# Another early order for all five engines of a routed attention and expert kernel, with a few early copies on other engines

## The chip, the cores and the metric

The kernel runs on one core of a Trainium2 chip. The core has five engines that run their own instruction lists in order and meet through semaphores: PE (TensorE, matmuls; its weight loads are shown apart as PEld), DVE (VectorE), ACT (ScalarE), POOL (GpSimd) and SP (SyncE, which here issues DMAs). The metric is device time in microseconds of one launch; a launch before the change took 225.79 us (median of 3 runs, 225.51 to 225.9).

## The reference

Attention in which a query sees only keys of its own cluster, then an expert layer on the result. Batch 4, 8 heads, 768 tokens, head size 64, 16 clusters; the expert layer takes 3072 tokens of 512 to 1024 and back.

```
q_assign = argmax(einsum('bhsd,hcd->bhsc', q_n, c_n))     # q_n, k_n, c_n: normalised rows
k_assign = argmax(einsum('bhsd,hcd->bhsc', k_n, c_n))
mask   = q_assign[:, :, :, None] == k_assign[:, :, None, :]
scores = where(mask, scale * q @ k.T, -1e9)
attn   = exp(scores - max);  attn = attn / (sum(attn) + 1e-9)
x      = (attn @ v).transpose(0, 2, 1, 3).reshape(3072, 512)
h      = x @ w_in
solu   = h * softmax(h)
out    = ((solu - mean) / sqrt(var + 1e-6) * g_ln) @ w_out
```

## The kernel before

Work goes by pairs of heads: b.p is batch b, pair p (two heads of 64 rows make 128 partitions), sixteen in all. For each pair queries (i = 0) and keys (i = 1) are loaded, turned so that the head dimension lies on partitions, cast to bf16 into a ring of six buffers qk (L469 ACT, L471 and L473 POOL or DVE), and 16 rows below them take the one-hot of each token's cluster, so that one matmul gives a score that is large only within a cluster. Pairs of batch 0 are loaded twelve tokens to a partition and turned by PE (tp, L404) and copied out of PSUM (xa, L431); pair 0.0 goes in two halves (L397, L423). In pairs 0.1 to 0.3 two tokens are interleaved, which the kernel calls two-token. Pairs of later batches are loaded in four pieces each (L437) and turned by DVE (xt, L445).

Clusters of a pair come in these steps, each a name in the tables: cl (PE, four matmuls, L487), tb (DVE, transpose back, L493), mx (DVE, maximum, L506), oh (DVE, compare, L519), ot (DVE, turn the one-hot, L525 for two-token pairs, L528 else), pl (place it in qk; L541 for two-token pairs, L548 else; four of them, keys 1.0 and 1.1 and queries 0.0 and 0.1) and bl (zeroes, L557). For two-token pairs cl is one pass of all 384 columns.

Attention: S is a bank of scores (PE, L635), E its exp (ACT, L643, nine buffers), V the product with the values (PE, L662, six matmuls), N the normalisation of a group of V (DVE, L674 and L687). Values are loaded by lv (L561) and cast by cv (L566). S0 to S3 are pair 0.0, S4 to S21 pairs 0.1 to 0.3, S22 is the first of batch 1.

Expert layer, by tiles f of 128 tokens: tx turns x (DMA, for tile 0 by PE as ptx0, L727, and a copy tx0), h is x @ w_in (L752; h0.0.0 the first), hm its maximum (DVE, L758), ex the exp (ACT, L764), u the product (DVE, L771), tu turns u (DMA), bn and ag the statistics (DVE), y the product with w_out (PE, L821; y0.0 the first), sc and ou the output. Weights before that: li and wi load and cast w_in (L586), lo loads w_out, su0 to su7 add its eight blocks, weighted by g_ln (DVE, L603 and L606), me0 and me1 take the column mean of that sum (PE, L612), ce0 to ce7 subtract it (DVE, L615).

The order of every engine is written out by hand. A table ORDER has one string for each engine: `E3 ex E11` means three E, one ex, eleven E, each time the next operation of that kind which belongs to this engine. A second table, AWAY, names operations that run on another engine than their default. `queues` takes the lists from these, and `run` records the operations so; it also has a cost model, but the order within an engine is the table's alone.

```
for kind, n in re.findall(r"([A-Za-z]+)(\d*)", text):
    for _ in range(int(n or 1)):
        queues[e].append(of[e, kind].pop(0))
```

Needs between operations (`needs` in each `add`) become semaphore waits. An engine that meets a wait stops there: nothing behind it in its list runs.

Of the kernel before, what the change touches and what calls it, by code (L numbers as in the profile page):

```python
# [22 lines left out]
class Weave:  # L23
# [5 lines left out]
    ORDER["SP"] = """
        ld4 si ld3 lv lg ld2 lv lo ld lv2 lo ld10 lo2 ld2 li4 ld4 lv ld tx ld2 tx ld lv tu ld10 tx  # L30
        tu ld4 tu lv ld ou lv ld3 tu ld3 ou ld8 ou2 ld2 tu ld5 tx lv2 ld pl tu ld10 tx ld5 ou2 tu lv
        tx lv tu ld9 ou tu ld4 lv2 ld4 pl tu ou tx ld3 tu tx ld4 ou tu2 ou lv tx lv ou pl3 tu3 ou
        tx2 ou2 tu tx tu tx tu ou2 tx ou tu2 ou tu ou6
    """
# [7 lines left out]
    ORDER["PE"] = """
        fl wm tp2 cp fl3 tp cl tp fl tp fl4 cl tp3 fl S2 cq tp S2 cl S2 tp S2 tp S tp S gt V3 S tp S
        cl V3 S2 tp S2 tp S3 tp S V S V2 S7 V2 S V S2 cl S2 V2 S V S3 V S3 V3 S V S2 cl S4 V2 S V2
        S4 V4 S5 me V S2 V2 S V me S3 V S ptx V3 S3 V S2 V h2 V S V S h S2 h S V S V S V2 cl S3 V2
        h2 S V S h V S h S h S h V S2 V2 S y3 V S2 y S h2 S2 V2 h2 S2 cl S V S V2 S V S h S2 h S V S
        V S h y4 S3 V3 h2 S2 V2 S h S2 V y S y3 S2 V2 S cl S V S V S V2 S2 y S y S2 V3 S2 y S V S y
        S2 V2 S h S2 V3 S2 cl S V3 S3 cl S2 V2 S V2 S h2 S3 h V S V S V2 y3 S2 y V S2 V h S2 V S h S
        V S h2 S3 h V2 S2 V4 h S3 y3 S2 V y S2 V3 S2 h2 S3 V2 cl S3 V2 h S2 h cl V2 S2 V2 S h S2 h2
        S2 V3 y S y S y S y V S V2 S h2 S2 h2 S3 V3 S V y3 V y V S2 h S cl S3 V2 h S2 h V S2 V S cl  # L50
        V2 S3 y2 S V S V y2 h2 S2 V2 S h2 S3 cl S V3 S V S2 y3 S2 V y V S h S2 h V2 S h2 S3 h V2 S
        y2 S V2 S2 V2 y2 S2 h3 S3 V2 h2 V y S3 y3 V3 S3 h2 S2 cl S V S V S V2 S y2 h V S2 h V S2 h2
        S2 V S V h V4 S2 y2 h S3 V2 h2 S2 V2 S y2 S2 h2 y2 S h2 S2 V2 y S V2 S y h2 S3 h2 S2 V4 y S3
        h2 y V S2 h2 V S V S V y4 S2 V h4 S3 y V3 y S2 y2 h4 y S V3 y V y2 h ptx h y h2 y3 h2 y4 h2
        ptu2 y8 ptu y4 ptu y4
    """
    ORDER["DVE"] = """
        cn xb cb ca tb mx oh ot pl2 tb mx oh bl cf ot xa bl tb pl xa mx gk xa oh ot cv pl tb mx N oh
        xa2 su cv ot su2 N tb xt mx oh N xt su ot N pl tb mx su N su3 N oh xt ot N ce2 tx N ce5 N xt
        hm N ce u tb mx bn N hm oh bn ot ag u xt2 hm cv N bn u bn2 tb mx hm bn N oh ag2 u ot xt2 hm  # L60
        bn N sc u bn tb ag cv N xt mx oh xt ot sc N bl xt2 tb bn N mx ca tb N mx oh ot hm oh N ot u
        xt bn3 ag xt N ag hm sc N ca u bn2 xt bl sc hm ag N xt tb mx u tb oh ot N hm mx xt oh u bn2
        ot N hm bn ag xt ca u N bn tb xt2 mx ag hm tb N bn2 oh ot u xt2 N hm tb mx oh N ag bn bl u
        mx bn ot N bn oh hm ot ag xt u N bn xt ag hm bn2 ag u sc N bl hm ca tb mx cv2 oh u ot N bn2
        hm N bl u cv ag bn2 hm N bn u sc hm N u bn2 hm N bn ag u bn sc hm ag N bn u bn2 hm bn N ag2
        u bn2 hm ag bn N ag2 u tx bn hm sc u bn2 hm tu2 bn ag2 u2 bn2 ag tu sc
    """
# [16 lines left out]
    AWAY.update(dict.fromkeys("""
        ca0.0.1.1.0 ca0.0.1.1.1 pl0.0.0.0.0 pl0.0.0.1.0 pl0.0.1.1.0 pl1.0.0.0 pl1.0.0.1 pl1.0.1.0
        pl1.0.1.1 pl1.1.0.0 pl1.1.0.1 pl1.1.1.0 pl1.1.1.1 pl1.2.0.0 pl1.2.0.1 pl1.2.1.0 pl1.2.1.1
        pl1.3.0.0 pl1.3.0.1 pl1.3.1.0 pl1.3.1.1 pl2.0.0.0 pl2.0.0.1 pl2.0.1.0 pl2.0.1.1 pl2.1.0.0
        pl2.1.0.1 pl2.1.1.0 pl2.2.0.0 pl2.2.0.1 pl2.2.1.0 pl2.2.1.1 pl2.3.0.0 pl2.3.0.1 pl2.3.1.0
        pl2.3.1.1 pl3.0.0.0 pl3.0.0.1 pl3.0.1.0 pl3.1.0.0 pl3.1.0.1 pl3.1.1.0 pl3.1.1.1 pl3.2.0.0
        pl3.2.0.1 pl3.2.1.0 pl3.2.1.1 pl3.3.0.0  # L90
    """.split(), "POOL"))
# [1238 lines left out]
```

## Time and profile before

| | |
|---|---|
| time, median of 3 runs | 225.79 us (225.51 to 225.9) |
| profiled execution, its own time | 224.72 us |
| span of the profile | 222.9 us |
| ACT: exps, L643 | 142.7 us in 276 |
| PE: scores, L635 | 89.0 us in 600 |
| PE: values, L662 | 55.0 us in 1152 |
| PE: x @ w_in, L752 | 48.4 us in 177 |
| PE: u @ w_out, L821 | 45.1 us in 169 |

The span runs from the first to the last instruction; the time of the execution has what lies around it, 1.8 us here. Busy time is the sum over instructions, where overlaps count once. A row of a timeline has start, length, engine, line, operation and tiles, and in brackets the idle time of the engine just before it with what ended it. A wait for several semaphores is put down to the one that came last.

### The profile page before, as it was taken

What the parts mean: (1) busy time and instruction counts of PE and PEld (TensorE: products, weight loads), DVE (VectorE), ACT (ScalarE), POOL (GpSimd) and SP (SyncE); (2) the same over time, 40 slices, a digit from 0 to 9 for tenths busy, and PEclk for the clock granted to TensorE, in tenths of its full rate; (3) what the DMA queues carried; (4) which work ended last, traced back from release to release, by engine and by line L of the source; (5) the groups of instructions that cost most, each with busy time, mean ns of one, the idle gap of its engine ahead of it and who ended that gap; (6) DMA issues with size and microseconds to landing.
All of it is one profiled execution on the core that took longest, in us unless ns stands there. A gap on an engine that the chain in (4) does not pass through costs nothing.

```text
span 222.9 us, 6842 instructions
## 1 busy us (share of the span) xinstructions
PE 213.3 (96%) x2518; PEld 150.0 (67%) x2548; DVE 200.7 (90%) x365; ACT 194.1 (87%) x379; POOL 127.1 (57%) x246
## 2 busy tenths in 40 slices
...
GB/s 164 345 364 197 117 247 328 157 183 151 132 168 188 244 169 203 144 198 155 164 224 225 177 218 95 150 158 162 230 102 46 107 90 144 115 164 122 167 97 143
DMA packets 122433, 38.74 MB, mean 174 GB/s; under 512 B 111448, under 2 KB 117152, under 8 KB 122400
## 3 DMA queue, kind: packets, MB, share of 16 engines
...
## 4 chain that ended last, share of the span: by engine, by line
PE 80%; DVE 7%; POOL 3%; issue 3%; DMA 3%; ACT 2%; SPq 0%; DVEq 0%; POOLq 0%; ACTq 0%
PE sps L635 24%; PE hreg L752 18%; PE yps L821 17%; PE ops L662 14%; PE csc L487 4%; DMA raw<-in_q_dram 3%; DVE w_sum L606 2%; POOL qk L471 2%; POOL qk L541 1%; PE hreg L404 1%; DVE xt L445 1%; ACT xt L431 1%; PE hreg L821 1%; ACT e L643 1%; DVE w_out_c L615 1%
## 5 line engine op out<-in xcount | busy, mean ns | idle before, releaser
L643 ACT ACTIVATE e<-sps 128x512 bf16<-128x512 f32 (+1 forms) x276 | 142.7, 602 | 11.1 <-PE sps L635 10.4
L635 PE MATMUL sps<-qk 80*128 80x256 bf16 (+5 forms) x600 | 89.0, 263 | 2.2 <-POOL qk L541 1.8
L635 PEld LDWEIGHTS <-qk 80*128 80x128 bf16 (+1 forms) x636 | 59.6, 121 | 25.3 <-issue 10.6
L662 PEld LDWEIGHTS <-e 128*128 128x128 bf16 x1152 | 50.0, 97 | 10.9 <-DVE x L687 2.5
L662 PE MATMUL ops<-v,e 128*128 128x65 bf16 x1152 | 55.0, 193 | 0.7 <-DVE x L687 0.5
L752 PE MATMUL hreg<-w_in_sb,xT 128*128 128x512 bf16 x177 | 48.4, 378 | 0.8
L821 PE MATMUL yps<-w_out_c,uT 128*128 128x512 bf16 x169 | 45.1, 379 | 0.8
L548 POOL COPY qk<-oht 32x384 f32<-32x384 f32 (+1 forms) x48 | 23.9, 498 | 15.6 <-DVE oht L528 9.4
L782 DVE BATCH_NORM_STATS2 bs<-u 128x6 f32<-128x512 bf16 x48 | 31.4, 678 | 0.0
L771 DVE TENSOR_TENSOR u<-e_sb,hreg 128x1024 bf16<-128x1024 bf16 (+1 forms) x25 | 29.1, 1167 | 2.6 <-ACT e_sb L764 1.9
L764 ACT ACTIVATE e_sb<-hreg,nmax 128x1024 bf16<-128x1024 f32 x24 | 26.9, 1121 | 4.5 <-DVE nmax L758 4.4
L758 DVE TENSOR_REDUCE nmax<-hreg 128x1 f32<-128x1024 f32 x24 | 29.1, 1211 | 1.4 <-PE hreg L752 1.2
L798 POOL TENSOR_SCALAR esq<-es,mv 128x1 f32<-128x1 f32 x24 | 8.2, 340 | 37.3 <-DVE mv L786 34.2
L821 PEld LDWEIGHTS <-uT 128*128 128x128 bf16 x200 | 18.0, 97 | 13.1 <-issue 0.3
L471 POOL CAST qk<-xt 64x768 bf16<-64x768 f32 (+1 forms) x28 | 23.2, 828 | 4.6 <-ACT xt L423 3.2
L473 POOL TENSOR_SCALAR qk<-xt 64x768 bf16<-64x768 f32 (+1 forms) x29 | 23.4, 808 | 3.6 <-DVE xt L445 1.7
L752 PEld LDWEIGHTS <-xT 128*128 128x128 bf16 x192 | 17.5, 97 | 11.1 <-DVE u L771 0.7
L445 DVE STREAM_TRANSPOSE xt<-raw 128x768 f32<-128x768 f32 x24 | 22.4, 950 | 0.0
L687 DVE TENSOR_TENSOR x<-ops,den 128x256 bf16<-128x256 f32 (+1 forms) x39 | 18.9, 486 | 1.3
L792 POOL TENSOR_SCALAR es<-esum 128x1 f32<-128x1 f32 x24 | 5.4, 230 | 19.6 <-ACT e_sb L764 19.1
L801 POOL TENSOR_TENSOR alpha<-esq,halves 128x1 f32<-128x1 f32 x24 | 13.7, 573 | 2.0
L838 ACT ACTIVATE y<-yps,alpha 128x512 f32<-128x512 f32 x15 | 10.4, 694 | 4.3 <-PE yps L821 3.0
...
## 6 DMA issues: line engine op xcount, KB each, us to landing
...
```

Source lines behind the costliest of these rows:

```text
L445: nc.vector.transpose(xt[:], raws[b, p, i][:].rearrange("p j c -> p (j c)"))
L471: VEC[e].tensor_copy(dst, src)
L548: ins = VEC[e].tensor_copy(dst.bitcast(F32), src.bitcast(F32).unsqueeze(1) .to_broadcast([NB, 2, n // 2]))
L635: ins = nc.tensor.matmul(sps_[n, k][:, c0:c0 + w], side(b, h // 2, 1, h % 2, keys)[r], side(b, h // 2, 0, h % 2, slice(s0 * P, s0 * P + w) ...
L643: ins = nc.scalar.activation(es[n, k][:, :w], sps_[n, k][:, :w], Act.Exp, scale=exp_scale, bias=-exp_scale)
L662: nc.tensor.matmul(opss[g][:, s, :VW], es[n, k][:, c0:c0 + P], v1[slot(b, h // 2)][:, h % 2, kt, :VW], start=(kt == 0), stop=(kt == n_t - 1))
L752: uses(nc.tensor.matmul(hreg[:, at(f, f2)[1], :], xTs[f][:, dc, :], w_in_sb[:, dc, f2 * FF2:(f2 + 1) * FF2], start=(dc == 0), stop=(dc == ...
L758: uses(nc.vector.tensor_reduce(ff[f, "nmax"][:], pair_of(f), axis=AXY, op=Alu.max, negate=True), *both(f))
L764: uses(nc.scalar.activation(ff[f, "e"][:], pair_of(f), Act.Exp, bias=ff[f, "nmax"][:], accum_out=ff[f, "esum"][:]), *both(f))
L771: uses(nc.vector.tensor_tensor(ff[f, "u"][:, r], ff[f, "e"][:, r], pair_of(f)[:, r], op=Alu.mult), *both(f)[r])
L782: nc.vector.bn_stats(ff[f, "bs"][:, f2, :], ff[f, "u"][:, f2, :])
L821: ins = nc.tensor.matmul(dst, ff[f, "uT"][:, at(f, f2)[0] * (n_fc // 2) + c, :], w_out_c[:, fc, cols], start=(fc == fcs[0] and turn == 0 i ...
```

## The change

The text of the program outside the two tables is the same word for word: the same operations, the same matmuls, the same single pass of clusters for two-token pairs. The strings of ORDER differ from their start to a place in the early part of the program, about where tile 2 of the expert layer starts (PE: ahead of V23.0; DVE: ahead of u1; ACT: ahead of E22.1; POOL: ahead of pl1.1.1.0; SP: ahead of ld1.2.1.1); behind it they are equal. AWAY moves some early copies:

- to ACT: ca0.0.0.1.1 (from DVE), ca0.1.1.1 (from POOL), tx0, xa0.2.0.0, xa0.2.1.0, xa0.2.1.1 and xa0.3.0.1 (from DVE)
- to DVE: ca0.0.1.0.1, xa0.1.1.1, xa0.2.0.1, xa0.3.0.0 and xa0.3.1.0 (from ACT), ca0.2.0.1, cv0.0.0, cv0.0.1, cv0.3.1 and cv1.0.1 (from POOL); pl0.0.0.0.0 (from POOL)
- to POOL: ca0.2.1.0 and ca1.1.0.1 (from ACT), bl0.0.0, cv0.1.0, cv0.1.1, pl0.0.0.1.1, pl0.1.1.1 and pl0.3.1.0 (from DVE)

```diff
-        S4 V4 S5 me V S2 V2 S V me S3 V S ptx V3 S3 V S2 V h2 V S V S h S2 h S V S V S V2 cl S3 V2
+        S2 V S3 V2 S2 V2 S2 me S me V ptx S V S V S2 V S cl V S V S h S V h S2 V S h S h S2 V3 S h V
...
-        ca0.0.0.0.0 ca0.2.1.0 ca1.1.0.1 ca3.2.0.1 sc23.0 xa0.0.0.1 xa0.0.1.0 xa0.1.0.0 xa0.1.0.1
-        xa0.1.1.0 xa0.1.1.1 xa0.2.0.1 xa0.3.0.0 xa0.3.1.0 xb0.0.1.1
+        ca0.0.0.0.0 ca0.0.0.1.1 ca0.1.1.1 ca3.2.0.1 sc23.0 tx0 xa0.0.0.1 xa0.0.1.0 xa0.1.0.0
+        xa0.1.0.1 xa0.1.1.0 xa0.2.0.0 xa0.2.1.0 xa0.2.1.1 xa0.3.0.1 xb0.0.1.1
     """.split(), "ACT"))
```

The first two lines are PE's, around the column means: four V and three S stand between the two `me` before, and only one S now. `cl`, the clusters of pair 1.1, come ahead of the first h.

Three places in the built programs. A row names the line, the operation, what it writes and reads, and the shape; `x3` stands for three equal rows.

POOL, from the last placement of pair 0.0 (qk_99) to the placements of pair 0.2 (qk_101; qk_100 is pair 0.1, qk_102 pair 0.3), before:

```order
L548 COPY qk_99<-oht 32x2x96
L566 CAST v_0_105<-vf 128x6x64
L541 COPY qk_100<-w_out_c 16x2x3x64
L471 CAST qk_101<-xt 64x6x128 x2
L541 COPY qk_100<-w_out_c 16x2x3x64 x2
L473 TENSOR_SCALAR qk_101<-xt 64x6x128
L541 COPY qk_101<-w_out_c 16x2x3x64
L471 CAST qk_102<-xt 64x6x128 x2
```

And of the change:

```order
L548 COPY qk_99<-oht 32x2x96
L471 CAST qk_101<-xt 64x6x128
L473 TENSOR_SCALAR qk_101<-xt 64x6x128 x2
L541 COPY qk_100<-w_out_c 16x2x3x64 x4
L566 CAST v_1_106<-vf 128x6x64
L471 CAST qk_102<-xt 64x6x128
L1295 MEMSET v_3_108 128x12x2
L566 CAST v_1_106<-vf 128x6x64
L471 CAST qk_102<-xt 64x6x128
```

The casts of pair 0.2 now stand ahead of the first placement of pair 0.1 and those of pair 0.3 ahead of the first placement of pair 0.2; all four placements of pair 0.1 are POOL's and follow each other.

DVE, around the last weighted sums (w_sum), with normalisations (L674, L687), the one-hot of pair 1.0 (oh) and the turn of pair 1.1's queries (xt), before:

```order
L606 SCALAR_TENSOR_TENSOR w_sum<-w_g,g_ln_115,w_sum 128x512 x3
L674 RECIPROCAL den<-ops 128x4
L687 TENSOR_TENSOR x<-ops,den 128x2x2x64
L519 TENSOR_TENSOR oh<-cst,mx 128x384
L445 STREAM_TRANSPOSE xt<-raw 128x768
```

And of the change:

```order
L445 STREAM_TRANSPOSE xt<-raw 128x768
L606 SCALAR_TENSOR_TENSOR w_sum<-w_g,g_ln_115,w_sum 128x512
L674 RECIPROCAL den<-ops 128x4
L687 TENSOR_TENSOR x<-ops,den 128x2x2x64
L606 SCALAR_TENSOR_TENSOR w_sum<-w_g,g_ln_115,w_sum 128x512
L519 TENSOR_TENSOR oh<-cst,mx 128x384
L606 SCALAR_TENSOR_TENSOR w_sum<-w_g,g_ln_115,w_sum 128x512
```

The last three sums (su5 to su7) stood together ahead of the normalisation N5; now the turn xt1.1.0, N5 and the one-hot stand ahead of the last of them.

ACT, from the exps of S14 to those of S17 (banks in hreg and sps), of the change:

```order
L643 ACTIVATE e<-sps 128x512 x3
L643 ACTIVATE e<-hreg 128x512
L731 COPY xT<-xtp 128x512
L643 ACTIVATE e<-hreg 128x512
L643 ACTIVATE e<-sps 128x512 x3
```

The copy tx0 (L731, on DVE at L733 before) now parts the two exps E15.2 and E16.0, which followed each other. On SP the loads of w_in (li) now come behind the four pieces of pair 1.1's keys, and all pieces of pair 1.0 and 1.1 stand further ahead among the loads of values and w_out.

More of the change, by code (lines that the diff above doesn't have):

```diff
@@ L29 @@
     ORDER["SP"] = """
[L30 to L33, printed above, removed]
+        ld4 si ld3 lv lg ld4 lo ld2 lv ld lo lv ld4 lv lo ld6 lo ld2 li4 ld tx lv tx ld2 lv ld2 tu
+        ld9 tx tu ld4 tu lv ld ou lv ld3 tu ld3 ou ld8 ou2 ld2 tu ld5 tx lv2 ld pl tu ld10 tx ld5
@@ L34 @@
+        ou2 tu lv tx lv tu ld9 ou tu ld4 lv2 ld4 pl tu ou tx ld3 tu tx ld4 ou tu2 ou lv tx lv ou pl3
+        tu3 ou tx2 ou2 tu tx tu tx tu ou2 tx ou tu2 ou tu ou6
     """
     ORDER["POOL"] = """
-        po ca3 pl z2 pl ca3 pl2 ca cv ca z pl cv pl ca2 pl2 ca pl ca2 pl z pl2 cv2 ca cv ca pl sg ca
-        pl2 wi cv wi4 pl wi pl wi ca pl wi pl bl ca2 cv2 at ca al cv pl2 ca3 at pl2 z bl ca3 al at
-        al pl4 at ca cv ca cv ca cv al bl ca3 pl4 ca2 pl4 at2 pl2 bl ca cv pl al2 ca2 cv2 ca2 at cv
@@ L39 @@
-        ca4 al pl4 at2 cv bl cv3 pl2 al pl2 ca2 bl ca at al ca pl2 cv2 pl ca3 al ca3 pl at2 pl3 al2
-        ca2 pl ca at cv pl cv at ca at cv al pl2 bl pl al at3 al2 at al2 at al at al2 at3 al3
+        po ca pl2 ca bl z2 ca pl2 ca4 pl ca3 pl4 cv ca z cv ca sg pl3 z cv pl ca2 pl cv pl2 ca cv pl
+        wi ca wi7 ca pl4 ca cv2 ca2 bl at al pl2 ca3 at pl2 z bl ca3 al at al pl4 at ca cv ca cv ca
+        cv al bl ca3 pl4 ca2 pl4 at2 pl2 bl ca cv pl al2 ca2 cv2 ca2 at cv ca4 al pl4 at2 cv bl cv3
@@ L41 @@
+        pl2 al pl2 ca2 bl ca at al ca pl2 cv2 pl ca3 al ca3 pl at2 pl3 al2 ca2 pl ca at cv pl cv at
+        ca at cv al pl2 bl pl al at3 al2 at al2 at al at al2 at3 al3
     """
     ORDER["PE"] = """
-        fl wm tp2 cp fl3 tp cl tp fl tp fl4 cl tp3 fl S2 cq tp S2 cl S2 tp S2 tp S tp S gt V3 S tp S
-        cl V3 S2 tp S2 tp S3 tp S V S V2 S7 V2 S V S2 cl S2 V2 S V S3 V S3 V3 S V S2 cl S4 V2 S V2
-        S4 V4 S5 me V S2 V2 S V me S3 V S ptx V3 S3 V S2 V h2 V S V S h S2 h S V S V S V2 cl S3 V2
@@ L46 @@
[L46 to L55, printed above, removed]
+        fl wm tp2 cp fl3 cl tp2 fl5 tp2 cl fl S tp S cq S tp S2 tp2 S3 cl S2 tp2 V3 S2 gt tp2 S2 V3
@@ new lines @@
+        S cl S2 tp S2 tp S2 V2 S V S4 cl S V3 S6 V2 S2 V S V S3 V S V2 S2 V S2 cl S V S V S V2 S4 V3
+        S2 V S3 V2 S2 V2 S2 me S me V ptx S V S V S2 V S cl V S V S h S V h S2 V S h S h S2 V3 S h V
+        S2 h V2 S2 h V S2 V S h S h V2 h S2 V S y3 V S2 y S h2 S2 V2 h2 S2 cl S V S V2 S V S h S2 h
+        S V S V S h y4 S3 V3 h2 S2 V2 S h S2 V y S y3 S2 V2 S cl S V S V S V2 S2 y S y S2 V3 S2 y S
+        V S y S2 V2 S h S2 V3 S2 cl S V3 S3 cl S2 V2 S V2 S h2 S3 h V S V S V2 y3 S2 y V S2 V h S2 V
@@ new lines @@
+        S h S V S h2 S3 h V2 S2 V4 h S3 y3 S2 V y S2 V3 S2 h2 S3 V2 cl S3 V2 h S2 h cl V2 S2 V2 S h
+        S2 h2 S2 V3 y S y S y S y V S V2 S h2 S2 h2 S3 V3 S V y3 V y V S2 h S cl S3 V2 h S2 h V S2 V
+        S cl V2 S3 y2 S V S V y2 h2 S2 V2 S h2 S3 cl S V3 S V S2 y3 S2 V y V S h S2 h V2 S h2 S3 h
+        V2 S y2 S V2 S2 V2 y2 S2 h3 S3 V2 h2 V y S3 y3 V3 S3 h2 S2 cl S V S V S V2 S y2 h V S2 h V
+        S2 h2 S2 V S V h V4 S2 y2 h S3 V2 h2 S2 V2 S y2 S2 h2 y2 S h2 S2 V2 y S V2 S y h2 S3 h2 S2
@@ L56 @@
+        V4 y S3 h2 y V S2 h2 V S V S V y4 S2 V h4 S3 y V3 y S2 y2 h4 y S V3 y V y2 h ptx h y h2 y3
+        h2 y4 h2 ptu2 y8 ptu y4 ptu y4
     """
     ORDER["DVE"] = """
[L58 to L66, printed above, removed]
+        cn xb cb tb mx oh ot pl ca pl tb mx oh ot xa pl cf bl xa cv tb cv mx oh ca gk xa ot su N tb
@@ new lines @@
+        xa mx xa oh ot su tb N mx su oh xt N xt ot su N cv tb su mx N xt su N su oh su N xt ce3 N
+        ce4 ot ce N hm tb N u mx bn2 N cv hm oh ag ot u xt2 hm cv N bn u bn2 tb mx hm bn N oh ag2 u
+        ot xt2 hm bn N sc u bn tb ag cv N xt mx oh xt ot sc N bl xt2 tb bn N mx ca tb N mx oh ot hm
+        oh N ot u xt bn3 ag xt N ag hm sc N ca u bn2 xt bl sc hm ag N xt tb mx u tb oh ot N hm mx xt
+        oh u bn2 ot N hm bn ag xt ca u N bn tb xt2 mx ag hm tb N bn2 oh ot u xt2 N hm tb mx oh N ag
@@ L67 @@
+        bn bl u mx bn ot N bn oh hm ot ag xt u N bn xt ag hm bn2 ag u sc N bl hm ca tb mx cv2 oh u
+        ot N bn2 hm N bl u cv ag bn2 hm N bn u sc hm N u bn2 hm N bn ag u bn sc hm ag N bn u bn2 hm
+        bn N ag2 u bn2 hm ag bn N ag2 u tx bn hm sc u bn2 hm tu2 bn ag2 u2 bn2 ag tu sc
     """
     ORDER["ACT"] = """
-        wa xa2 ca xa ca xb xa2 ca xa3 E9 xa E3 xa ca E7 xa E57 ex E3 ca E5 ex E5 sc E3 ex E11 ex E3
-        sc E5 ex E35 ex E15 ex E15 ex E9 ex E3 sc E8 ex sc E14 ex E sc E10 ex E5 sc E6 ex E5 sc E3
@@ L71 @@
-        ex ca E10 ex E9 ex E5 sc E2 ex E6 ex E7 ex E6 ex sc E5 ex E3 sc E ex sc ex sc ex sc2 tu sc2
-        oz
+        wa xa2 ca xa2 xb ca2 xa2 E xa E4 xa E4 ca xa E3 xa2 E48 tx E15 ex E9 ex E5 sc E3 ex E11 ex
+        E3 sc E5 ex E35 ex E15 ex E15 ex E9 ex E3 sc E8 ex sc E14 ex E sc E10 ex E5 sc E6 ex E5 sc
+        E3 ex ca E10 ex E9 ex E5 sc E2 ex E6 ex E7 ex E6 ex sc E5 ex E3 sc E ex sc ex sc ex sc2 tu
+        sc2 oz
     """
```

18 lines of the change are left out of this document (9 added, 9 removed).

## The prediction

> **What bounds the kernel now.** I read the page first, then the busy time by stretches of 5 us over the part whose order changes, then the chain of waits, then the rows of single engines where the chain turns.
>
> ```profile
> span 222.9 us, 6842 instructions
> PE 213.3 (96%) x2518; PEld 150.0 (67%) x2548; DVE 200.7 (90%) x365; ACT 194.1 (87%) x379; POOL 127.1 (57%) x246
> PE 80%; DVE 7%; POOL 3%; issue 3%; DMA 3%; ACT 2%; SPq 0%; DVEq 0%; POOLq 0%; ACTq 0%
> ```
>
> Over the whole program PE (TensorE) is the bound: 213.3 of 222.9 us busy, 80% of the chain. An order that leaves the matmuls alone can only win what PE stands idle.
>
> ```profile
> 25.00:30.00 5.00, 3.85 (x56) 2.53 (x49) 4.65 (x10) 5.00 (x11) 4.58 (x9) 1.00 0.78 120
> 30.00:35.00 5.00, 4.21 (x72) 2.96 (x69) 4.87 (x9) 4.97 (x11) 4.67 (x8) 1.00 1.08 289
> 35.00:40.00 5.00, 4.22 (x54) 3.22 (x54) 4.86 (x9) 4.42 (x10) 3.50 (x6) 1.00 1.02 360
> 40.00:45.00 5.00, 4.84 (x80) 4.04 (x79) 4.93 (x12) 4.91 (x11) 4.44 (x8) 1.00 0.79 129
> 55.00:60.00 5.00, 4.94 (x51) 3.43 (x50) 5.00 (x8) 4.95 (x11) 2.08 (x5) 1.00 0.79 128
> ```
>
> The columns after the length are busy PE, PEld, DVE, ACT, POOL. From 25 to 40 us PE works 3.85, 4.21 and 4.22 of each 5.00, so 2.7 us lie open there; from 55 on 4.94, next to nothing. The clock column is 1.00 throughout. DVE is at 4.65 to 5.00 in all five rows. So the prize is at most those 2.7 us and what the first ten add, and DVE decides how much can be had.
>
> ```profile
> 18.68 0.83 POOL qk L471
> ...
> 22.63 1.48 issue
> ...
> 28.51 0.38 PE sps L635 x2
> ...
> 29.67 0.97 DVE xt L445
> ...
> 37.79 0.98 DVE w_sum L606
> ...
> 44.24 0.36 PE ops L662 x6
> ```
>
> The chain of waits says who: POOL from 18.7 to 28.5, with a hole of 1.48 in it, then DVE from 29.7 to 44, then PE. After 44 us the chain is matmuls. The change must therefore be judged by when PE comes out of this passage.
>
> **The change part by part.** No instruction is added or removed but by engine: both programs issue four matmuls for each pass of clusters, since only the tables differ. What moves stands ahead of the third expert tile's first matmuls (h2.0.1, S24); from V23.0 on PE's order is the old one.
>
> *POOL.* It waits in order for two one-hot transposes of DVE (ot0.1, ot0.2), and PE then waits for the placements behind them (pl0.2, pl0.3).
>
> ```profile
> 18.12 0.50 POOL L541 COPY qk<-w_out_c 16x384 f32<-16x384 f32 x1 [1.56 <-DVE w_out_c L525]
> 24.12 0.93 POOL L541 COPY qk<-w_out_c 16x384 f32<-16x384 f32 x1 [1.50 <-DVE w_out_c L525]
> 28.51 0.38 PE L635 MATMUL sps<-qk 80*128 80x256 bf16 x2 [0.75 <-POOL qk L541]
> 35.27 0.38 PE L635 MATMUL sps<-qk 80*128 80x256 bf16 x2 [1.06 <-POOL qk L541]
> ```
>
> The new order puts three casts (0.83 each, the first row of the chain) ahead of pl0.1.1.0, where POOL stood 1.56 us. From there to pl0.2.0.0 it now has seven placements (0.50), two v casts and two memsets (each counted as a placement, which is more than they are) and two casts: 11x0.50+2x0.83, with 0.06 after each (18.62 to 18.68) 8.0 us. So pl0.2.0.0 ends at 18.1+8.0=26.1, and S8.0 has no wait at 28.5; pl0.3.0.0 stands seven short steps and two casts later, 5.7 us, at 31.8 instead of just ahead of 35.27. Both waits of PE, 0.75+1.06=1.81 us, go. What is late next is DVE.
>
> *DVE.* In the old order everything is dense from the first two-token transpose back (tb0.1) to the last of the eight weighted sums (su7), on which the column mean (me0, L612) waits.
>
> ```profile
> 13.37 0.22 DVE L557 MEMSET qk<- 16x192 f32 x1 [0.95 <-POOL qk L548]
> 29.11 0.18 DVE L674 RECIPROCAL den<-ops 128x4 f32<-128x4 f32 x1 [0.25 <-PE ops L662]
> 36.23 2.55 DVE L606 SCALAR_TENSOR_TENSOR w_sum<-w_g,g_ln,w_sum 128x512 f32<-128x512 f32 x3
> 38.70 0.17 DVE L674 RECIPROCAL den<-ops 128x4 f32<-128x4 f32 x1
> 39.24 0.87 DVE L519 TENSOR_TENSOR oh<-cst,mx 128x384 bf16<-128x384 f32 x1
> 40.03 0.97 DVE L445 STREAM_TRANSPOSE xt<-raw 128x768 f32<-128x768 f32 x1
> 40.92 0.53 DVE L528 STREAM_TRANSPOSE oht<-oh 128x384 bf16<-128x384 bf16 x1
> L471 DVE CAST qk<-xt 64x768 bf16<-64x768 f32 x2 | 1.1, 549 | 0.0
> L541 DVE COPY qk<-w_out_c 16x384 f32<-16x384 f32 x2 | 1.2, 590 | 0.1
> L431 DVE COPY xt<-hreg 128x384 f32<-128x384 f32 x5 | 2.6, 542 | 0.0
> L548 DVE COPY qk<-oht 32x192 f32<-32x192 f32 x3 | 1.1, 354 | 0.1
> ```
>
> Between tb0.1 and su7 the new list has four operations more: one cast (0.55), N5 (38.70 to 39.24, 0.54), the one-hot of pair 1.0 (39.24 to 40.03, 0.79) and xt1.1.0 (40.03 to 40.92, 0.89), together 2.77. It has four fewer: two placements (2x0.59), one copy out of PSUM (0.54), one small placement (0.35), together 2.07; the two v casts that leave and the two that come cancel. Net 0.70 longer. The idle 0.25 at 29.11 goes, as PE is ahead there. Where tb0.1 starts is not shown: it loses the wait of 0.95 for POOL but now stands behind cl0.1, which PE starts later; between 0.95 earlier and 0.5 later I take 0, the old place. So su7 ends at 38.78+0.70-0.25=39.2, about when it did.
>
> *PE behind me0.* This is the term that pays.
>
> ```profile
> 38.83 0.70 PE L612 MATMUL hreg<-w_sum,g_mean 128*128 128x256 f32 x2 [0.42 <-DVE w_sum L606]
> 39.38 0.36 PE L662 MATMUL ops<-v,e 128*128 128x65 bf16 x6
> ...
> 40.82 0.67 PE L612 MATMUL hreg<-w_sum,g_mean 128*128 128x256 f32 x2
> ...
> 56.99 1.24 PE L821 MATMUL yps<-w_out_c,uT 128*128 128x512 bf16 x5
> ```
>
> Before, me0 at 38.83 leaves 56.99-38.83=18.16 us of work to the first output tile (y0.0). Four groups of V and three of S (V12, V13, S15) stood between me0 and me1, from 39.38 to 40.82: 1.44 us. Now they stand ahead of me0, all else behind it is the same set. PE gets them done there, because the 1.81 us of waits for POOL are gone and the 0.42 at me0 too. So y0.0 comes at 39.2+18.16-1.44=39.2+16.72=55.9 instead of 56.99: **1.1 us**.
>
> *The start* gives cover only.
>
> ```profile
> 9.32 1.20 PE L404 MATMUL hreg<-ident_f,raw 128*128 128x128 f32 x9
> ```
>
> S0.0, the first score, stood behind these nine transposes and three earlier ones; now six of the twelve stand ahead of it, so it may come 0.8 us sooner (six of nine in 1.20). I count this lead at nothing, since DVE takes it back; it is cover for the 1.44. If it does not come, up to 0.5 of that is missing.
>
> *ACT and SP.* The copy of the first x tile (tx0) goes from DVE to ACT, ahead of the exp of S16.0, where it waits for PE's ptx0 behind both column means.
>
> ```profile
> 41.32 1.10 ACT L643 ACTIVATE e<-hreg 128x512 bf16<-128x512 f32 x2
> 43.21 0.42 DVE L733 COPY xT<-xtp 128x512 bf16<-128x512 bf16 x1
> 37.57 0.66 POOL L586 CAST w_in_sb<-w_st 128x512 bf16<-128x512 f32 x1 [1.45 <-DMA w_st<-in_moe_w_in_dram]
> 45.28 0.81 PE L752 MATMUL hreg<-w_in_sb,xT 128*128 128x512 bf16 x3
> ```
>
> E16.0 is the second of the pair at 41.32, near 41.8. Now it follows me0 39.2+0.55 (38.83 to 39.38), S16.0 0.21 (seven groups in 1.44), me1 0.55, V14.0 and ptx0 0.21 each, and the copy 0.42: 41.35 and two handovers, no later than before, so nothing is lost; but any lead of ACT ends there. The casts of w_in (wi) wait for loads that now stand behind four more pieces of keys. POOL waited 1.45 us for them already; PE asks for the first at 45.28, nearly 8 us later. I count it at 0; the bounds are 0 and 1.45.
>
> From y0.0 on the order is the old one, and PE is full, so 1.1 us stay. DVE is lighter by 0.42 (tx0) behind me0; I add 0.1 for it. The profiled execution took 224.72 us, 222.9 of it span: 224.72-1.2=223.5. The median of the runs shown is 225.79, 1.07 above it; on that footing **224.6 us**.
>
> *A rule on ports.* The sums split: the three from 36.23, most of them while POOL waits for w_in up to 37.57, take 2.55 together, and the last of them, with POOL back at work, 0.98 of it (the chain's row). The Trainium skill, "SBUF — State Buffer", section "Who interferes with whom", says that a VectorE operation with two inputs in SBUF and a GpSimd operation that reads SBUF exclude each other for a whole instruction. The split agrees; by the page the time is that of the first rival, not the forecast's.
>
> **Rivals.**
> ```profile
> L606 DVE SCALAR_TENSOR_TENSOR w_sum<-w_g,g_ln,w_sum 128x512 f32<-128x512 f32 x7 | 6.1, 869 | 0.1
> L519 DVE TENSOR_TENSOR oh<-cst,mx 128x384 bf16<-128x384 f32 x12 | 7.1, 592 | 0.1
> ```
>
> *Sums beside an idle POOL.* In the new order POOL reaches wi0.0 one cast and two short steps behind pl0.3.0.0, near 33.8, and then waits for w_in until 37.57 or later, so su5 to su7 and the one-hot fall into that hole. Rows: the two sums ahead of the last take (2.55-0.98)/2=0.79 or less, the seven have a mean of 0.87, the one-hot 0.87 beside a mean of 0.59 over all twelve. If three sums save 0.1 each and the one-hot 0.28, me0 is 0.6 earlier: 224.0. Against it: su1 to su3 move beside a busier POOL. This is the result the port rule gives here.
>
> *Nothing arrives.* The lead is returned between me0 and y0.0: E16 late behind tx0, V16 waits for N7, the tile's u0 late. Since clusters and matmuls are the same, no other gain stands behind it: 225.8, from the point where these waits add 1.1 us. For it: DVE is at 4.93 of 5.00 there. Against it: E16.0 comes out at 41.35, ahead of its old 41.8.
>
> *The sums come late (slower).* The first sum (su0) moves ahead of the first normalisation and nearer to its w_out load, and all seven later sums may meet POOL. Price: a wait like the 1.45 for w_in, a load of the same size, and 7x(0.98-0.87)=0.77: me0 at 39.2+2.2=41.4. me0, me1, ptx0, tx0 and E16.0 are now one line, so everything follows: y0.0 at 41.4+16.72=58.1, 226.8. It is slower than before from me0 at 40.3.
>
> **How the numbers follow.** Forecast 0.58; sums beside an idle POOL 0.10 (224.0); nothing arrives 0.18 (225.8); sums late 0.14 (226.8). A measurement of this kernel tells about 0.2%, 0.45 us, from no change. The forecast's own bounds are tb0.1's start (0.95 earlier to 0.5 later) and the cover of 0.5: 223.7 to 225.5. Eight in ten needs the second rival and most of the third: 223.3 to 226.0. Faster 0.66, same 0.20, slower 0.14.
>
> **What would show it.** Right: POOL's waits for w_out_c L525 and PE's two for qk L541 are gone or under 0.3 us; me0 within 0.5 us of 39.2 with V13 and S15 ahead of it; the first yps at 55.9. Wrong: me0 after 40.3; ACT idle over 1 us ahead of the copy at L731; h0 waiting for w_in_sb; or y0.0 early and the end not, which would mean that the late order gives the lead back.

## The result and the profile after

The kernel before took 225.64 us (median of 20 runs, 224.95 to 226.13), the changed one **224.12 us** (median of 20 runs). The ratio is 0.9932, with a 95% interval of 0.9913 to 0.9951: 1.1 to 2.0 us off, 1.5 in the middle. The prediction said 1.2 off, 224.6, within 223.3 to 226.0. Medians here and below are over all runs, the ratios leave out runs more than 1.5% slower than the fastest of the same kernel (of these 20, those of 227.04 and 228.08 us).

The page of the changed kernel: span and instructions, busy time of each engine, and the chain by engine.

```profile
span 222.5 us, 6869 instructions
PE 214.3 (96%) x2548; PEld 149.6 (67%) x2548; DVE 199.4 (90%) x364; ACT 193.6 (87%) x379; POOL 127.3 (57%) x247
PE 86%; DMA 7%; DVE 2%; SPq 2%; ACT 1%; issue 0%; DVEq 0%; ACTq 0%
```

The 30 matmuls more than in the page before (2518) are no more work: that page lacks records (L752 x177 against x192 here, L821 x169 against x184). DVE fell from 7% of the chain to 2%, POOL from 3% to nothing, and DMA rose from 3% to 7%: in this execution, what sets the early passage has moved from POOL and DVE to the loads (4.0 us of a load of keys from 22.0, 5.3 us of one of w_out from 32.0). The same stretches as in the prediction (busy PE, PEld, DVE, ACT, POOL, then the clock, the DMA share and GB/s):

```profile
25.00:30.00 5.00, 4.14 (x68) 3.32 (x65) 4.97 (x9) 5.00 (x12) 4.58 (x8) 1.00 0.95 233
30.00:35.00 5.00, 4.43 (x68) 2.71 (x66) 4.93 (x11) 5.00 (x11) 4.64 (x8) 1.00 0.88 139
35.00:40.00 5.00, 4.11 (x58) 3.19 (x55) 4.14 (x10) 5.00 (x11) 0.05 (x1) 1.00 1.09 328
40.00:45.00 5.00, 5.00 (x74) 3.59 (x73) 4.96 (x9) 4.22 (x10) 3.78 (x7) 1.00 1.28 240
```

PE still stands 2.3 us between 25 and 40, against 2.7: most of the idle time is still there, and 0.81 us of it now lies just ahead of the column mean. The rows of the timeline that the prediction named (PE, DVE, ACT and POOL of the changed kernel, in order of time):

```profile
17.30 2.00 POOL L473 TENSOR_SCALAR qk<-xt 64x768 bf16<-64x768 f32 x2 [0.34 <-ACT xt L431]
19.35 2.16 POOL L541 COPY qk<-w_out_c 16x384 f32<-16x384 f32 x4
25.05 2.19 POOL L541 COPY qk<-w_out_c 16x384 f32<-16x384 f32 x3
27.29 0.38 PE L635 MATMUL sps<-qk 80*128 80x256 bf16 x2 [0.58 <-POOL qk L541]
35.17 0.71 DVE L606 SCALAR_TENSOR_TENSOR w_sum<-w_g,g_ln,w_sum 128x512 f32<-128x512 f32 x1
37.31 0.75 DVE L606 SCALAR_TENSOR_TENSOR w_sum<-w_g,g_ln,w_sum 128x512 f32<-128x512 f32 x1 [0.74 <-DMA w_g<-in_moe_w_out_dram]
37.98 0.55 DVE L519 TENSOR_TENSOR oh<-cst,mx 128x384 bf16<-128x384 f32 x1
38.45 0.74 DVE L606 SCALAR_TENSOR_TENSOR w_sum<-w_g,g_ln,w_sum 128x512 f32<-128x512 f32 x1
39.25 0.70 PE L612 MATMUL hreg<-w_sum,g_mean 128*128 128x256 f32 x2 [0.81 <-DVE w_sum L606]
41.06 0.59 ACT L731 COPY xT<-xtp 128x512 bf16<-128x512 bf16 x1 [0.78 <-PE xtp L727]
41.09 0.61 POOL L586 CAST w_in_sb<-w_st 128x512 bf16<-128x512 f32 x1 [6.04 <-DMA w_st<-in_moe_w_in_dram]
55.85 0.60 PE L821 MATMUL yps<-w_out_c,uT 128*128 128x512 bf16 x2
```

The first column mean (me0) starts at 39.25 and the first output tile (y0.0) at 55.85, as forecast (39.2, 55.9). But su6, the last sum but one, waits 0.74 us for the last load of w_out (lo3), PE waits 0.81 for the sums, ACT 0.78 behind that, and POOL 6.04 for w_in.

y0.0 is 1.14 us earlier than before, and the lead holds: the last store on SP is issued 1.15 earlier. Yet this profile's span is just 0.4 shorter. The last store (before, then after), and how long it took to land (last column of the DMA issues):

```profile
219.84 0.33 SPq L849 DMA_DIRECT2D out_dram<-w_in_sb  x1
out_dram<-w_in_sb SPq DMA_DIRECT2D x1, 160.0 KB, 1.8
```

```profile
218.69 0.33 SPq L849 DMA_DIRECT2D out_dram<-w_in_sb  x1
out_dram<-w_in_sb SPq DMA_DIRECT2D x1, 160.0 KB, 2.6
```

The store took 0.8 us longer in that one execution. So two single spans don't size this change; the runs do, and y0.0 within a profile.

### The profile page after: what moved, and what is told of

Same layout as the page of the kernel before. It is cut to its first block, busy times and chain, and to the rows that moved or that the text cites. A ratio compares the mean times of both kernels' runs of the same rounds, so it can differ in the third digit from the quotient of the medians.

```text
span 222.5 us, 6869 instructions
## 1 busy us (share of the span) xinstructions
PE 214.3 (96%) x2548; PEld 149.6 (67%) x2548; DVE 199.4 (90%) x364; ACT 193.6 (87%) x379; POOL 127.3 (57%) x247
## 4 chain that ended last, share of the span: by engine, by line
PE 86%; DMA 7%; DVE 2%; SPq 2%; ACT 1%; issue 0%; DVEq 0%; ACTq 0%
PE sps L635 25%; PE hreg L752 18%; PE yps L821 18%; PE ops L662 15%; PE csc L487 5%; DMA raw<-in_q_dram 3%; DMA w_g<-in_moe_w_out_dram 2%; DMA raw<-in_k_dram 2%; SPq L437 2%; PE hreg L404 1%; PE hreg L821 1%; DVE w_sum L606 1%; ACT e L643 1%; PE hreg L612 1%; PE hreg L635 0%
## 5 line engine op out<-in xcount | busy, mean ns | idle before, releaser
L752 PE MATMUL hreg<-w_in_sb,xT 128*128 128x512 bf16 x192 | 51.8, 379 | 0.0
L821 PE MATMUL yps<-w_out_c,uT 128*128 128x512 bf16 x184 | 47.4, 378 | 0.0
L821 PEld LDWEIGHTS <-uT 128*128 128x128 bf16 x200 | 18.0, 97 | 13.0 <-issue 0.3
L752 PEld LDWEIGHTS <-xT 128*128 128x128 bf16 x192 | 17.5, 97 | 10.7 <-DVE u L771 0.4
L687 DVE TENSOR_TENSOR x<-ops,den 128x256 bf16<-128x256 f32 (+1 forms) x39 | 19.0, 486 | 1.3
L792 POOL TENSOR_SCALAR es<-esum 128x1 f32<-128x1 f32 x24 | 5.9, 248 | 18.7 <-ACT e_sb L764 18.1
```

Source lines behind the costliest of these rows:

```text
L752: uses(nc.tensor.matmul(hreg[:, at(f, f2)[1], :], xTs[f][:, dc, :], w_in_sb[:, dc, f2 * FF2:(f2 + 1) * FF2], start=(dc == 0), stop=(dc == ...
L821: ins = nc.tensor.matmul(dst, ff[f, "uT"][:, at(f, f2)[0] * (n_fc // 2) + c, :], w_out_c[:, fc, cols], start=(fc == fcs[0] and turn == 0 i ...
```

## The experiments

Each kernel starts from the changed one, or from the one before where its label says so. Names are those of the tables. The ratio is to runs of the kernel before made beside each kernel. y0.0 is from the one profiled execution; a star marks profiles whose granted clock fell in the early part (see the last section).

| label | median, us | ratio to before | 95% interval | y0.0, us |
|---|---|---|---|---|
| changed kernel | 224.12 | 0.9932 | 0.9913 to 0.9951 | 55.85 |
| after_again (the same) | 224.19 | 0.9931 | 0.9911 to 0.9951 | 55.76 |
| me_back | 226.79 | 1.0049 | 1.0021 to 1.0078 | 57.33 |
| before_term | 226.04 | 1.0033 | 1.0007 to 1.0058 | 60.20* |
| before_term_n5 | 225.56 | 0.9996 | 0.9977 to 1.0015 | 57.73 |
| cover_gone | 226.72 | 1.0038 | 1.0016 to 1.0059 | 59.14* |
| cover_fill | 225.57 | 0.9990 | 0.9975 to 1.0006 | 57.19 |
| lo3_early | 223.65 | 0.9916 | 0.9894 to 0.9937 | 55.15 |
| lo3_again (the same) | 223.44 | 0.9899 | 0.9878 to 0.9919 | 58.37* |
| lo3_pool | 224.50 | 0.9951 | 0.9931 to 0.9971 | 55.64 |
| best2 | 224.13 | 0.9931 | 0.9911 to 0.9950 | 55.21 |
| tx0_dve | 224.31 | 0.9942 | 0.9917 to 0.9967 | 55.46 |
| lo3_tx0 | 224.23 | 0.9935 | 0.9911 to 0.9959 | 55.66 |

The start itself differs between executions: the first two-token transpose (tb0.1) lies between 13.4 and 14.4 us in the profiles without a star. A few tenths between two profiles are not read here.

### Is the gain the work moved ahead of the column means?

**me_back** puts the means back around that work:

```diff
-        S2 V S3 V2 S2 V2 S2 me S me V ptx S
+        S2 V S3 me V2 S2 V2 S2 me S V ptx S
```

> The changed kernel, with PE's two column means back around V12, V13, S14.2 and S15 (8 groups of 0.2 us, 1.64 us) instead of behind them. Theory (the gain is work moved from behind me0 to ahead of it): me0 stays at 39.2, PE stands idle ahead of it for 0.81+1.64 = 2.4 us, y0.0 comes at 39.2+16.6+1.6 = 57.4 instead of 55.85, and the time is 1.4 to 1.6 us above the changed kernel's 224.1: 225.6. Rival (the gain comes from what left DVE and ACT, and PE's order around the means is worth nothing): y0.0 within 0.3 of 55.85, time 224.1 to 224.3.

PE in its profile:

```profile
38.87 0.70 PE L612 MATMUL hreg<-w_sum,g_mean 128*128 128x256 f32 x2 [1.87 <-DVE w_sum L606]
39.40 0.54 PE L662 MATMUL ops<-v,e 128*128 128x65 bf16 x12
57.33 1.03 PE L821 MATMUL yps<-w_out_c,uT 128*128 128x512 bf16 x4
```

PE now stands 1.87 us ahead of me0, and y0.0 comes at 57.33: from me0 it is 18.46 us instead of 16.60, and 1.64 of these 1.86 us are the moved work (39.40 to 41.04). By y0.0 the whole gain is gone; the theory holds there. The median lies 1 us above the kernel before and above the 225.6 expected, for a reason that the last section gives.

**before_term** gives the kernel before this one thing alone:

```diff
-        S4 V4 S5 me V S2 V2 S V me S3 V S
+        S4 V4 S5 V S2 V2 S V me2 S3 V S
```

> The kernel before, with one thing of the change alone: V12, V13 and S15 (seven groups, 1.44 us) ahead of the first column mean on PE. Theory (the 1.44 us pay only where PE has a lead to do them in; before, PE waited just 0.42 us at me0, and V13 needs E13.2, which ACT ends at 38.9): me0 at 39.7 to 39.9 instead of 38.83, y0.0 at 39.8+16.72 = 56.5 instead of 56.99, time 0.3 to 0.5 below the kernel before: 225.3. Rival (the order around the means is worth its 1.1 us whatever stands ahead of it): y0.0 at 55.9, time 224.6. Second rival (worth nothing alone): 225.7.

Nothing is won: the ratio is 1.0033, slower if anything. In four of its twelve runs the clock fell; the other eight have 225.9 in the middle, which is nearest to the second rival. Ahead of V12.0, PE shows:

```profile
40.70 0.36 PE L662 MATMUL ops<-v,e 128*128 128x65 bf16 x6 [1.47 <-DVE x L687]
```

V12 reuses a PSUM tile that the normalisation N5 (L687) must have read, and in the old list of DVE N5 stands behind su7. So V12 cannot start before su7 has ended, which is all that me0 waits for: put ahead of me0, it only holds me0 back. The change moved N5 ahead of su7; the prediction counted that move only as time (0.54 us on DVE), not as the permission that the 1.44 us need.

**before_term_n5** adds it:

```diff
-        mx su N su3 N oh xt ot
+        mx su N su2 N su oh xt ot
```

> before_term once more, with the normalisation N5 ahead of the last sum (su7) on DVE, as in the change: there V12 waited 1.47 us for N5 and lost all. Theory (the gain needs both: N5 ahead of su7, and the lead that PE has from POOL's filled waits, which is missing here): no wait at V12.0, V13 and S15 done near 39.9, me0 at 39.9 to 40.0, y0.0 at 56.6 to 56.7, time 0.3 to 0.4 below the kernel before: 225.3. Rival (these two edits are the whole gain): y0.0 at 55.9, time 224.6. Second rival (worth nothing, or less): 225.7 or more.

```profile
39.23 0.36 PE L662 MATMUL ops<-v,e 128*128 128x65 bf16 x6 [0.45 <-DVE x L687]
40.67 1.11 PE L612 MATMUL hreg<-w_sum,g_mean 128*128 128x256 f32 x4
```

V12's wait falls to 0.45, but me0 slides to 40.67, 1.84 later than before, for 1.44 us of work moved ahead of it (0.37 of the 1.84 is there already at S12.0, at 35.64 instead of 35.27). Nothing is won, within 0.2%: the second rival. The two edits alone do not make the gain; that the lead of PE is what is missing is tested next, from the other side.

### Is that lead POOL's?

**cover_gone** takes 2.0 us of it away again, with two casts ahead of the last placements of pair 0.3:

```diff
-        ca2 pl cv pl2 ca cv pl wi ca wi7 ca pl4 ca
+        ca2 pl cv pl ca2 pl cv pl wi8 ca pl4 ca
```

> The changed kernel, with two casts of pair 1.0 (2.0 us) on POOL ahead of the last placements of pair 0.3, so that PE gets S12.0 about 2.0 us later, near 34.9. Theory (the lead that POOL's filled waits give PE is cover for V12, V13 and S15 ahead of me0, and 1.4 us of it, PE's waits of 0.56 at V10.0 and 0.81 at me0, are more than is needed): PE is done with S15.2 at 38.44+2.0-0.56 = 39.9, me0 at 39.9 instead of 39.25, y0.0 at 56.5, time 0.5 to 0.7 above: 224.7. Rival (PE's waits for POOL lie on the path in full): y0.0 at 57.8, time 226.1. Second rival (PE's early waits are worth nothing): time 224.1.

It lost 2.6 us instead of 0.6.

```profile
34.83 0.38 PE L635 MATMUL sps<-qk 80*128 80x256 bf16 x2 [1.82 <-POOL qk L541]
```

S12.0 waited 1.82 us and came at 34.83, as meant; but then the clock fell. Busy PE and the columns behind it in 2-us stretches of cover_gone:

```profile
33.00:35.00 2.00, 0.18 (x3) 0.16 (x2) 1.97 (x5) 1.45 (x3) 1.85 (x3) 1.00 0.95 295
35.00:37.00 2.00, 1.72 (x28) 1.49 (x27) 1.08 (x2) 1.61 (x4) 1.38 (x2) 0.95 1.15 244
37.00:39.00 2.00, 2.00 (x21) 1.60 (x19) 1.37 (x4) 1.97 (x4) 0.00 (x0) 0.50 1.00 341
39.00:41.00 2.00, 2.00 (x27) 1.71 (x25) 1.03 (x2) 1.64 (x4) 0.43 (x1) 0.50 1.02 406
41.00:43.00 2.00, 2.00 (x10) 1.43 (x8) 1.49 (x3) 1.19 (x3) 1.89 (x4) 0.50 0.58 161
```

**cover_fill** keeps that order and lets PE work through most of the wait:

```diff
+        for _ in range(28 if (n, k) == (12, 0) else 0):
+            nc.tensor.matmul(sps_[n, k][:, :P], ident_b[:], ident_b[:])
```

> cover_gone once more, with 28 matmuls of 128 columns ahead of S12.0 into its own bank (the scores then start the bank anew), so that PE works through some 1.6 us of the 1.82 us that it waited for POOL there; S12.0 comes no earlier. In cover_gone's profile the granted clock fell to 0.50 from 37 to 43.5 us, behind that wait. Theory (the wait itself costs 0.5 to 0.7 us, as expected of cover_gone, and the rest of its 2.6 us is the clock that a standing PE loses): clock 1.00 throughout, V13 and S15 done at 39.9, me0 at 39.9, y0.0 at 56.5, time 224.7, no single run above 225.6. Rival (the wait costs it all, the clock falls for another reason): time 226 to 227 as in cover_gone, with clocks below 0.99.

```profile
33.36 1.73 PE L633 MATMUL sps<-ident_b 128*128 128x128 bf16 x28
35.30 0.38 PE L637 MATMUL sps<-qk 80*128 80x256 bf16 x2 [0.21 <-POOL qk L541]
37.78 0.18 DVE L676 RECIPROCAL den<-ops 128x4 f32<-128x4 f32 x1 [1.25 <-PE ops L664]
39.47 0.75 DVE L606 SCALAR_TENSOR_TENSOR w_sum<-w_g,g_ln,w_sum 128x512 f32<-128x512 f32 x1
```

```profile
37.00:39.00 2.00, 1.92 (x30) 1.53 (x30) 1.18 (x3) 1.91 (x5) 0.00 (x0) 1.00 1.00 375
```

The first fence has PE and DVE, in order of time, the second one stretch (line numbers behind 631 are two higher in this kernel). In this profile the clock stays at 1.00, and 1.15 us of the 2.6 come back in the median with S12.0 no earlier (35.30): so much was the clock. The four runs of cover_gone in which it did not fall agree (225.57 to 225.73). Five of cover_fill's twelve runs lie above the limit of 225.6 that was expected, two of them far: 228.09 us, with a mean clock of 0.998, so not for the clock, and 247.05 us, with one of 0.851, which stays unexplained.

The other 1.4 us are the wait itself, over twice what was expected, and why so much stays open in part. PE and DVE are both late at me0. On PE, S12.0 comes 2.43 us later than in the changed kernel's profile (35.30 against 32.87), not 2.0, and me0 at 40.27, not 39.9. On DVE, N5 waits 1.25 us for PE's V11, and as N5 now stands ahead of su6 and su7, the sums wait behind it; su7 starts at 39.47 instead of 38.45 and ends at 40.22, within some 0.1 us of the end of what PE has ahead of me0. So the change made the sums depend on PE, but this profile does not show that this cost more than PE's own list. From me0 to y0.0 it is 0.3 us longer as well (16.92). POOL's lead is in any case worth at least what the prediction said.

### What bounds the changed kernel: the last load of w_out

**lo3_early**, and the same kernel again as **lo3_again**, move one load by two places on SP:

```diff
-        ld4 lv lo ld6 lo ld2 li4 ld tx
+        ld4 lv lo ld4 lo ld4 li4 ld tx
```

> The changed kernel, with the last load of w_out (lo3) two pieces of keys earlier on SP, so that those two pieces land behind it. Theory (su6 waits 0.74 us for lo3, and me0 hangs on it): the wait goes, su7 ends near 38.5, me0 at 38.5, where PE is just done with S15.2 (38.44); ACT's hole of 0.78 ahead of tx0 goes too; y0.0 at 55.1, time 223.4, and the single times lie closer together. Rival (PE, ACT or the loads of w_in, which do not come earlier, take the place): h0.0.1 (wi3.0 ends at 46.05) or the copy tx0 waits, y0.0 at 55.6 or later, time 224.0 or more.

> lo3_early as it was, for its interval. Theory (su6 never waits for lo3 now, and PE never stands long enough for the clock to fall): median 223.6 to 223.8, no single run over 224.8, all clocks 0.995 or more. Rival (the first six runs were lucky): median 224.1, with runs over 226.

DVE and PE in lo3_early's profile:

```profile
35.21 0.71 DVE L606 SCALAR_TENSOR_TENSOR w_sum<-w_g,g_ln,w_sum 128x512 f32<-128x512 f32 x1
36.52 0.74 DVE L606 SCALAR_TENSOR_TENSOR w_sum<-w_g,g_ln,w_sum 128x512 f32<-128x512 f32 x1
37.65 0.75 DVE L606 SCALAR_TENSOR_TENSOR w_sum<-w_g,g_ln,w_sum 128x512 f32<-128x512 f32 x1
38.45 0.70 PE L612 MATMUL hreg<-w_sum,g_mean 128*128 128x256 f32 x2
55.15 1.03 PE L821 MATMUL yps<-w_out_c,uT 128*128 128x512 bf16 x4
```

The wait is gone, me0 starts at 38.45 without one, y0.0 at 55.15: to a tenth what was expected. The medians are 0.5 and 0.7 us below the changed kernel's and 0.8 and 1.0% below the kernel before: **lo3_early beats the kernel before clearly**, and the changed kernel by medians of few runs whose intervals overlap. One of its twelve runs took 226.94, at a mean clock of 0.992, so the expected limits of 224.8 and 0.995 held for eleven. That run is the one profiled as lo3_again, and it shows another wait of PE: 1.61 us for a load of keys, up to 11.70 us. PE there (busy PE, clock, DMA share, GB/s):

```profile
10.00:15.00 5.00, 3.34 (x20) 0.84 1.05 350
15.00:20.00 5.00, 5.00 (x47) 0.82 0.70 166
```

me0 and y0.0 come 3.2 us later than in lo3_early (41.66 and 58.37). In lo3_early's profile ACT is now full:

```profile
35.00:40.00 5.00, 4.92 (x70) 3.76 (x67) 4.87 (x11) 5.00 (x12) 1.10 (x3) 1.00 0.97 239
40.00:45.00 5.00, 4.95 (x69) 3.38 (x68) 4.96 (x9) 5.00 (x12) 3.37 (x6) 1.00 1.08 266
```

**after_again** runs the changed kernel once more.

> The changed kernel as it is, on the same chip as the other three, for the spread of its single times. Theory (in some executions lo3 lands early enough and su6 does not wait, in others it waits up to 0.8 us and more): median 224.1, single times from 223.0 to 225.0, su6's wait and me0 (38.5 to 39.3) differ from profile to profile by the same amount, and a few runs over 226 have a clock below 0.995. Rival (the spread is that of the last stores or of the clock alone): su6's wait is again 0.7 and me0 39.25 within 0.1.

In this execution su6 did not wait at all (its row shows no bracket), me0 started at 38.99 and y0.0 at 55.76; the start was 0.2 later there (tb0.1 at 13.93), and the first sum waited 0.47 for its own load instead of 0.24. DVE came to su6 0.5 us later there (37.06, where it stood ready at 36.57), but lo3 had also landed at least 0.25 earlier than the 37.31 of the first profile. So when lo3 lands differs between executions, as the theory has it; part of the spread is the start. y0.0 is just 0.1 earlier without the wait, so what lo3 costs is read from lo3_early's medians and not from these two profiles.

**best2** also moves a sum (su4) behind the turn xt1.1.0:

```diff
-        N cv tb su mx N xt su N su oh
+        N cv tb mx N xt su2 N su oh
```

> lo3_early with one sum (su4) behind the turn xt1.1.0 on DVE, so that N4 and xt1.1.0 come a sum earlier and su4 falls nearer to the stretch in which POOL stands. Theory (su4 takes 0.75 to 0.85 there instead of 1.03; N4 comes 0.5 earlier and PE's wait of 0.37 at V10.0 goes; but V13 still waits for E13.2, which ACT, full since 10 us, ends no earlier): me0 at 38.2 to 38.4, y0.0 0.1 to 0.2 earlier, time 223.4 to 223.6. Rival (DVE and PE alone set me0): me0 at 38.1, y0.0 at 54.8, time 223.3. Second rival (xt1.1.0 meets its load in some executions): 223.8 or more.

PE's wait at V10.0 went, and me0 did not move (38.44, y0.0 at 55.21): DVE and PE alone do not set me0, which fits V13 behind ACT's exps. The median is half a microsecond above lo3_early's, though; its profile shows no wait of xt1.1.0 for its load, and why it is slower stays open.

### Do the sums feel POOL?

**lo3_pool** is lo3_early with two casts in the hole in which POOL waits for w_in:

```diff
-        ca cv pl wi ca wi7 ca pl4 ca cv2
+        ca cv pl ca2 wi8 pl4 ca cv2
```

> lo3_early once more, with two casts of pair 1.0 (ca1.0.0.1, ca1.0.1.0; 0.82 each) on POOL ahead of its wait for w_in, where it stood 3.8 us, so that they lie beside su5, N5 and su6. Theory (su5 to su7 take 0.71 to 0.75 instead of 0.95 to 1.03 only because POOL stands still beside them): su5 near 0.95, su6 0.8 to 1.0, su7 unchanged, me0 0.3 to 0.5 later, at 38.8 to 38.9, PE waits there 0.3 to 0.5, y0.0 at 55.5 to 55.7, time 0.3 to 0.5 above lo3_early's 223.65: 224.0 to 224.1. Rival (the sums do not depend on POOL; w_in comes out earlier): su5 at 0.71, y0.0 at 55.15 or earlier, time 223.4 to 223.7.

POOL and DVE of lo3_pool, against lo3_early's three sums above:

```profile
34.90 0.82 POOL L471 CAST qk<-xt 64x768 bf16<-64x768 f32 x1
34.96 1.31 DVE L606 SCALAR_TENSOR_TENSOR w_sum<-w_g,g_ln,w_sum 128x512 f32<-128x512 f32 x1
35.80 1.16 POOL L473 TENSOR_SCALAR qk<-xt 64x768 bf16<-64x768 f32 x1
36.74 0.76 DVE L606 SCALAR_TENSOR_TENSOR w_sum<-w_g,g_ln,w_sum 128x512 f32<-128x512 f32 x1
37.76 1.70 POOL L586 CAST w_in_sb<-w_st 128x512 bf16<-128x512 f32 x2 [0.80 <-DMA w_st<-in_moe_w_in_dram]
37.89 1.09 DVE L606 SCALAR_TENSOR_TENSOR w_sum<-w_g,g_ln,w_sum 128x512 f32<-128x512 f32 x1
```

The sum that starts beside a cast takes 1.31 instead of 0.71, the one that starts beside a cast of w_in 1.09 instead of 0.75, the one between them 0.76. The cast that starts beside the first sum is longer too, 1.16 us against 0.82 of the one ahead of it. The theory holds, with me0 at 39.04 and y0.0 at 55.64; the median rose by 0.85 to 1.06 us, more than the 0.3 to 0.5 expected. POOL's wait for w_in (3.83 us in lo3_early, 6.04 in the changed kernel) is no loss here; filling it costs. This fits the rule of the Trainium skill ("SBUF — State Buffer", section "Who interferes with whom") that the prediction weighed: a DVE instruction with two inputs in SBUF contends with a GpSimd instruction that reads SBUF.

### Does the copy tx0 on ACT cost or pay?

**tx0_dve** puts it back on DVE in the changed kernel, **lo3_tx0** in lo3_early:

```diff
-        su N xt ce3 N ce4 ot
+        su N xt ce tx ce2 N ce4 ot
```

> The changed kernel, with the copy of the first x tile (tx0) back on DVE, behind ce0; ACT's exps E15.2 and E16.0 follow each other again. Theory (E16.0 loses nothing behind tx0, since PE is what limits from me0 on): E16.0 earlier by up to 1.0 us (at 40.4 to 40.6 instead of 41.54), ce1 to ce7 0.4 later, y0.0 within 0.2 of 55.85, time 224.1 within 0.2. Rival (tx0 on ACT costs its hole of 0.78 on the path): y0.0 at 55.2 to 55.4, time 223.4 to 223.6. Second rival (the 0.42 off DVE is worth its time): y0.0 at 56.2, time 224.5.

> lo3_early with the copy tx0 back on DVE, behind ce0. Theory (ACT and PE are both full behind me0, and the 0.4 us of tx0 is worth as much to the one as to DVE): y0.0 within 0.2 of 55.15, time 223.5 to 223.9. Rival (ACT is what limits there): E16.0 at 40.0 and all behind it 0.4 earlier, y0.0 at 54.7, time 223.2. Second rival (tx0 off DVE was worth its 0.42): y0.0 at 55.6, time 224.1.

PE of tx0_dve, at V16.0 (line numbers are one lower in that kernel):

```profile
43.01 0.36 PE L661 MATMUL ops<-v,e 128*128 128x65 bf16 x6 [0.17 <-DVE x L686]
```

E16.0 did come 1.4 us earlier (40.15 instead of 41.54, su6 not waiting in that execution), but y0.0 follows me0 no sooner: with tx0 on DVE, V16 waits 0.17 us for N7, in both kernels. From me0 to y0.0 it is 16.84 and 17.15 us instead of 16.60 and 16.70; the second execution of the changed kernel, after_again, has 16.77. The medians are 0.2 and 0.6 to 0.8 us higher; the intervals overlap. By the time, tx0_dve came out as its theory had it and lo3_tx0 as its second rival. So ACT is not the bound behind me0; whether tx0 off DVE is worth more than the 0.1 counted is not settled.

## Why the prediction was right, and where it was not

- **The term that pays** (step on PE behind me0): right in place and size. Forecast y0.0 at 55.9, found 55.85; me_back takes all of it back.
- **What allows it**: only half told. The forecast rested the term on PE's lead from POOL. It needs that (cover_gone, cover_fill), and N5 ahead of su7: where N5 stands behind su7, V12 waits for it (before_term). N5's new place without the lead does not pay (before_term_n5); the lead without N5's new place was not run.
- **POOL**: its two waits for the one-hot transposes are gone, as said (in after_again 0.49 us of one is left). But pl0.2.0.0 ended at 27.24 and pl0.3.0.0 at 32.81, 1.1 and 1.0 later than worked out. The lists themselves were as long as added up (19.35 to 27.24 is 7.9 us against 8.0, and from there 5.6 against 5.7), with some placements longer (pl0.2.1.1 0.86 against 0.50) and the memsets shorter. What was wrong is where they begin: the prediction left pl0.1.1.0 at its old 18.1, and it started at 19.35, since the three casts put ahead of it run from 15.93 to 19.29, two of them longer than 0.83 (ca0.2.0.0 1.03, ca0.2.1.1 1.11) and with a wait of 0.34 for a copy of ACT. So of PE's 1.81 us, 0.58 stayed, over the 0.3 named as a sign, and the second wait went, just in time (S12.0 at 32.87). At me0 PE now waits 0.81, where it was 0.42.
- **The start**: S0.0 came 1.0 us earlier (9.48 against 10.47), where 0.8 was counted on as cover.
- **DVE**: me0 at 39.25 against 39.2 is luck, two errors that cancel. Without its waits the list from tb0.1 to su7 took 24.5 us, where 25.6 was added up. Of this 1.1, at least 0.6 is in the last three sums and the one-hot, which took 0.71, 0.75, 0.74 and 0.55 beside an idle POOL, where 2.55 for the three and 0.79 for the one-hot were counted. And two waits for loads, counted at nothing, put 1.0 back: 0.24 at su0 and 0.74 at su6, for lo3. The rival "sums beside an idle POOL" was right about the sums. The rival "sums come late" was right that a load of w_out would hold them, but put it at su0 (0.24), with a price too large for what came.
- **ACT and SP**: E16.0 at 41.54 (forecast 41.35, before 41.81), nothing lost; h0.0.0 at 44.24 without a wait, so the late w_in cost nothing, though POOL waited 6.04 for it.
- **The size**: 1.2 us forecast, 1.5 measured, with an interval of 1.1 to 2.0. The difference lies inside the interval. Executions in which su6 does not wait have me0 earlier than forecast (38.99 in after_again, 38.62 in tx0_dve, which is the same up to there), which would account for some of it; that it does is not shown.
